# Scores of the second and third batch as row tiles, by head, with a new order of steps

## The chip, the core and the metric

The kernel runs on one core of one Trainium2 chip. The metric is the device time of one execution in microseconds (us). The engines are named as in the profile: PE (TensorE) multiplies, PEld is its loading of weights, ACT (ScalarE) and DVE (VectorE) read PE's results out of PSUM, POOL (GpSimd) and SP (SyncE) mostly issue DMAs.

## What is computed

A sliding-window causal attention (window 64) over 8 batches, 8 heads, 576 positions and a head size of 64, and after it a layer of its own kind on the 4608 tokens:

```python
scores = q @ k.T / 8, masked to 0 <= row - col < 64
x      = softmax(scores) @ v               # (8, 576, 512) -> 4608 x 512
h      = x @ w_in                          # 512 -> 2048
out    = (h - tanh(h)) @ w_out             # 2048 -> 512
```

## The kernel before

**Units.** A batch's 576 positions are 9 windows of 64. Heads go in pairs: pair `g` is batch `g // 4`, heads `g % 4` and `g % 4 + 4`; g = 0 to 3 are the first batch, 4 to 7 the second, 8 to 11 the third, and so on. The two layers work on chunks `c` of 512 tokens, 9 in all; chunk 0 needs only the first batch.

**The first three batches** are turned on PE. A pair's q or k is loaded as 96 partitions by 768 values (GpSimd's loads turn float32 into bfloat16 on the way; pair 0 comes as float32 by SP), cast or rearranged by ACT or DVE into a tile where the two heads lie side by side (`cast`), transposed on PE in six pieces (`tr`, line 253) and copied from PSUM (`put`, through `move`, line 88 on ACT and 90 on DVE). A pair that isn't cast is transposed directly, in twelve half-width pieces (line 249); pairs 2 and 3 are. k lands in `kT[g % 2]`. For the first batch q lands in `qp`, one copy with head a in partitions 0 to 63 and head b in 64 to 127, and its scores are 18 matmuls on 64 rows of the array, one for each window and head (line 286), in two groups of 4 and 5 windows; the mask is added by a product with `hide` (line 281). For the second and third batch q lands twice, in halves of `qT`, which is zero elsewhere: one matmul over 128 rows then gives a window's scores for both heads (line 292), in three groups of three windows; there the mask is a product on DVE after the exp (`masking`, line 329). Then come exp on ACT (`probs`, line 324), PV on PE (line 341 for the first batch, 354 for two pairs together later), the norm on DVE, and transposes of the result into a chunk (`x_tr`, line 403, and `x_put`).

**The other five batches** are loaded by tokens (line 159), transposed by DMAs on SP's queue (lines 164 and 172) and need no PE transposes; their scores (line 310, with 305 for the last window) are row tiles already.

**The layers.** `first_layer` is four matmuls of 512 columns for each of 16 row blocks `m` of a chunk (line 437), `tanh` on ACT (445), `subtract` on DVE (451) into `gT`; `yp_mm` is the second layer (line 480, and 473 for the last block), `y_out` copies a result from PSUM and stores it by SP (496).

**Order.** Nothing is scheduled by a program: `PLAN` is a list of steps in the order in which they are recorded, and each engine runs its own instructions in that order. A step is a letter code with numbers, looked up in `STEPS`. `lk.g`, `lq.g` load a pair's k and q; `LV`, `lv`, `lt` load v; `lr`, `qr` load k and q by tokens, `tk`, `tq` transpose them; `wi`, `wo` load the weights. `ck`, `cq` cast; `Fp.g.b` and `Ep.g.b` transpose k and q into PSUM bank `b`; `Fc` copies k, `Ec`, `Ea`, `Eb` copy q; `Rp.g.n.b` are scores of group `n`, `Rx` their exp, `M` the mask product; `Z`, `za`, `zb` copy v between halves of the partitions; `P`, `PP` are PV, `D`, `DS`, `DH`, `DR`, `DN` norms; `Xp`, `Xc` and `Y` bring x into a chunk. `H.c.m`, `A.c.m`, `G.c.m` are first layer, tanh and subtraction, `W.c.s.p` a quarter of the second layer of 128 tokens, `O.c.s` its output; `S.g` and `Sx.g` are the scores and exps of two pairs of the later batches. `U.n.b` is `n` dummy matmuls of 512 columns into bank `b`, in holes of PE's work. A last letter names the engine: p POOL, a ACT, v DVE, s SP.

The tile framework adds the waits. Three kinds matter here: a PSUM bank is written again only when its reader is done; `kT` and `qp` have two buffers, so pair g + 2 waits until pair g's scores are through; and GpSimd's DMAs take eight semaphores in turn, so one is issued only when the one eight before it has landed.

Of the kernel before, what the change touches and what calls it, by code (L numbers as in the profile page):

```python
# [15 lines left out]
def kernel(  # L16
# [200 lines left out]
    def warm_up(n, bank=5):  # L217
        w = 3 if bank == 6 else 4
        for i in range(n):
            nc.tensor.matmul(ps[:, bank, 0:128 * w], warm, warm.unsqueeze(1).to_broadcast([128, w, 128]), start=True, stop=True)  # L220
# [52 lines left out]
    def scores(g, grp, bank):  # L273
# [4 lines left out]
        if g // NP in BY_HEAD:  # L278
            if not first:
                for h in range(2):  # L280
                    nc.tensor.matmul(sp[:, :, h], ident, hide[:, h].unsqueeze(1).to_broadcast([128, n, 64]),  # L281
                                     start=True, stop=False)
            for i, j in enumerate(js):
                for h in range(2):
                    r = slice(64 * h, 64 * h + 64)
                    nc.tensor.matmul(sp[:, i, h], kt[r, 64 * j:64 * j + 128], qp[g % NKR][r, 64 * j:64 * j + 64],
                                     start=first, stop=first or i == n - 1)
            return
        if not first:
            nc.tensor.matmul(sp, ident, hide.unsqueeze(1).to_broadcast([128, n, 2, 64]), start=True, stop=False)  # L290
        for i, j in enumerate(js):
            nc.tensor.matmul(sp[:, i], kt[:, 64 * j:64 * j + 128], qT[g % NR][:, :, 64 * j:64 * j + 64],  # L292
                             start=first, stop=first or i == n - 1)
# [347 lines left out]
```

## Time and profile before

| | us |
|---|---|
| median of 3 runs | 312.18 (311.56, 312.18, 312.53) |
| the profiled execution | 311.42 |
| its span, first to last instruction | 309.7 |
| PE busy in the span | 301.3 (97%) |
| DVE, ACT, POOL busy | 183.7, 156.2, 103.0 |
| first and second layer on PE (lines 437, 480) | 140.4 and 134.3 |
| mean granted clock of PE | 0.989 of full |

Times inside the kernel are counted from the start of the span. In rows of groups the numbers after the bar are the busy time in us, the mean of one instruction in ns, and the idle time of its engine before it with what ended that. In the timeline the first two numbers are the start and the length. PE's matmuls overlap and their ends are modelled, so distances between starts tell more than lengths: a matmul of 512 columns has a length of 380 ns, but four of them take 0.86 us.

### The profile page before, as it was taken

What the parts mean: (1) busy time and instruction counts of PE and PEld (TensorE: products, weight loads), DVE (VectorE), ACT (ScalarE), POOL (GpSimd) and SP (SyncE); (2) the same over time, 40 slices, a digit from 0 to 9 for tenths busy, and PEclk for the clock granted to TensorE, in tenths of its full rate; (3) what the DMA queues carried; (4) which work ended last, traced back from release to release, by engine and by line L of the source; (5) the groups of instructions that cost most, each with busy time, mean ns of one, the idle gap of its engine ahead of it and who ended that gap; (6) DMA issues with size and microseconds to landing.
All of it is one profiled execution on the core that took longest, in us unless ns stands there. A gap on an engine that the chain in (4) does not pass through costs nothing.

```text
span 309.7 us, 6275 instructions
## 1 busy us (share of the span) xinstructions
PE 301.3 (97%) x2522; PEld 159.8 (52%) x2522; DVE 183.7 (59%) x321; ACT 156.2 (50%) x266; POOL 103.0 (33%) x139
## 2 busy tenths in 40 slices
...
GB/s 151 132 176 199 197 182 187 181 169 141 145 137 162 148 117 151 164 155 125 159 160 177 161 179 117 89 134 35 3 70 110 34 35 34 34 34 36 37 65 102
DMA packets 133436, 37.33 MB, mean 121 GB/s; under 512 B 122016, under 2 KB 127904, under 8 KB 133408
## 3 DMA queue, kind: packets, MB, share of 16 engines
...
q8 instruction: 19, 0.31, 0.4%
...
## 4 chain that ended last, share of the span: by engine, by line
PE 89%; DVE 3%; POOL 3%; DMA 2%; issue 1%; ACT 1%; POOLq 0%; ACTq 0%; DVEq 0%
PE ps L480 39%; PE ps L437 38%; PE ps L354 3%; PE ps L310 2%; DMA qall<-in_q_dram 2%; POOL vw L143 1%; PE ps L253 1%; DVE gT L451 1%; PE ps L473 1%; PE ps L292 1%; PE ps L403 1%; DVE qt L90 1%; PE ps L281 1%; POOL kall L108 1%; ACT th L445 1%
## 5 line engine op out<-in xcount | busy, mean ns | idle before, releaser
L451 DVE TENSOR_TENSOR gT<-ps,th 128x512 bf16<-128x512 f32 x144 | 97.7, 687 | 79.6 <-ACT th L445 79.0
L437 PE MATMUL ps<-xT,wi 128*128 128x512 bf16 x576 | 140.4, 380 | 0.5 <-DVE gT L451 0.2
L445 ACT ACTIVATE th<-ps 128x512 f32<-128x512 f32 x144 | 85.2, 598 | 100.0 <-PE ps L437 98.6
L480 PE MATMUL ps<-w_out_sb,gT 128*128 128x512 bf16 x560 | 134.3, 380 | 0.0
L437 PEld LDWEIGHTS <-wi 128*128 128x128 bf16 x576 | 63.0, 114 | 54.7 <-issue 0.9
L480 PEld LDWEIGHTS <-gT 128*128 128x128 bf16 x560 | 53.7, 98 | 60.9
L143 POOL DMA_DIRECT2D vw<-in_v_dram x35 | 30.5, 882 | 16.6 <-DVE q L90 9.0
L159 POOL DMA_DIRECT2D kall<-in_k_dram x25 | 21.6, 877 | 26.0 <-DMA kw<-kall 24.9
L159 POOL DMA_DIRECT2D qall<-in_q_dram x25 | 21.8, 879 | 20.9 <-DMA qw<-qall 17.5
L320 ACT ACTIVATE pt<-ps 128x1024 bf16<-128x1024 f32 (+1 forms) x30 | 23.3, 812 | 6.1 <-PE ps L310 5.9
L88 ACT ACTIVATE ysb<-ps 128x512 f32<-128x512 f32 (+1 forms) x20 | 11.6, 582 | 24.8 <-PE ps L480 19.7
L90 DVE COPY ysb<-ps 128x512 f32<-128x512 f32 (+1 forms) x17 | 11.6, 680 | 20.2 <-PE ps L480 19.5
L329 DVE TENSOR_TENSOR pt<-pt,ps 128x1152 bf16<-128x1152 bf16 x28 | 20.5, 746 | 3.2 <-ACT pt L320 2.8
L324 ACT ACTIVATE pt<-ps 128x384 bf16<-128x384 f32 (+2 forms) x32 | 16.9, 528 | 5.3 <-PE ps L292 3.4
L374 DVE TENSOR_TENSOR xs<-ps,rcp 128x384 bf16<-128x384 f32 x28 | 14.8, 550 | 0.2
L354 PEld LDWEIGHTS <-pt 128*64 128x64 bf16 x504 | 9.1, 111 | 5.1 <-issue 1.6
L354 PE MATMUL ps<-vw,pt 128*64 128x65 bf16 x504 | 10.7, 197 | 0.0
L220 PE MATMUL ps<-warm 128*128 128x512 bf16 x27 | 9.2, 498 | 1.1 <-DVE warm L197 1.1
L88 ACT ACTIVATE kt<-ps 128x576 bf16<-128x576 bf16 x10 | 6.5, 648 | 6.5 <-PE ps L253 3.5
L108 POOL DMA_DIRECT2D kall<-in_k_dram x11 | 7.3, 668 | 3.2 <-DMA wi<-in_moe_w_in_dram 1.8
...
L292 PE MATMUL ps<-qt,kt 128*128 128x128 bf16 x72 | 8.0, 219 | 0.0
...
## 6 DMA issues: line engine op xcount, KB each, us to landing
...
w_out_sb<-in_moe_w_out_dram POOLq DMA_DIRECT2D x4, 512.0 KB, 10.1
kall<-in_k_dram POOLq DMA_DIRECT2D x11, 144.0 KB, 5.2
qall<-in_q_dram POOLq DMA_DIRECT2D x11, 144.0 KB, 7.2
...
```

The source lines that it names most:

```text
L88: nc.scalar.activation(o, i, ACT.Copy)
L143: nc.gpsimd.dma_start(out=w[:, 2 * i + 1, :, 0:D] if i < NF else w[64:128, 2 * i, :, 0:D], in_=v[b, :, 128 * i:128 * i + n].rearrange("h p ...
L159: nc.gpsimd.dma_start(out=token_rows(b, n)[0:c, i], in_=(q if n == "q" else k)[b, :, 128 * i:128 * i + c].rearrange("h p d -> p h d"))
L320: nc.scalar.activation(o, sp, ACT.Exp, scale=scale)
L324: nc.scalar.activation(PT[g % NPT][:, js[0]:js[0] + len(js), :].rearrange("p i (h t) -> p i h t", h=2), sp, ACT.Exp, scale=scale)
L329: nc.vector.tensor_tensor(p, p, mask.unsqueeze(1).to_broadcast([128, 2 * NJ, 64]), ALU.mult)
L354: nc.tensor.matmul(ps[r, bank, 65 * i:65 * i + 65], PT[(g + r2) % NPT][:, j, r], vw[b % 2][:, j, p0 + r2 + NP * h, :], start=True, stop=True)
L374: nc.vector.tensor_tensor(xs[b % 2][:, 0:6, p0 + n // 2, :], ov[:, :, 0:D], sums[g][:, n].to_broadcast([128, 6, D]), ALU.mult)
L437: nc.tensor.matmul(hp, w_in_tile(ki, m), chunk_tile(c)[:, n.start // 64:n.stop // 64, ki % 2, 64 * (ki // 2):64 * (ki // 2) + 64], start=( ...
L445: nc.scalar.activation(th[:, n], hp, ACT.Tanh)
L451: nc.vector.tensor_tensor(gT[c][:, m, columns(s)], hp, th, ALU.subtract)
L480: nc.tensor.matmul(yp, gT[c][:, m, s * 128:(s + 1) * 128], w_out_sb[:, m, :], start=n == 1 and i == 0, stop=n == 4 and i == 3)
```

## The change

- The scores of the second and third batch are made as those of the first: row tiles by head, two groups of 5 and 4 windows for a pair, each head's scores in a bank of its own, from one copy of q (`qp`). `qT`, its two fills with zero (`pads_q`) and the steps `Ea` and `Eb` go. The mask stays a product after the exp.
- Pair 1 is no longer cast (`ck.1`, `cq.1`): it is transposed directly, as pairs 2 and 3 were.
- A new step `Hp` (`first_layer_part`) makes half of a first-layer block, for one half of the heads; blocks 0 to 2 of chunk 0 use it, so a block can start when two of the four pairs of x are there.
- The dummies are single steps in more places: 35 matmuls instead of 27.
- The whole list stands in a new order; which engine copies what changes too (24 of 37 y copies on ACT instead of 20).

In the new file the lines are: 215 dummies, 244 and 248 transposes, 269 `hide`, 274 row-tiled scores, 287 and 292 scores of later batches, 306 exp, 419 first layer, 491 its halves.

```diff
@@ -60,7 +60,6 @@
     WIDE = 512, 512, 1024
     w_in_sb = [const.tile([128, 4, n], BF16, name=f"wi{i}") for i, n in enumerate(WIDE)]
     w_out_sb = const.tile([128, M, d_model], BF16, name="w_out_sb")
-    BY_HEAD = (0,)
     NR, NPT, NROW = 2, 4, 3
     NKR = NR
     hidden_by_product = range(4)
@@ -72,7 +71,6 @@
     PT = [PT_all[:, i] for i in range(NPT)]
     kT = [const.tile([128, 64 + S], BF16, name=f"kt{i}") for i in range(NKR)]
     kw = [const.tile([128, NP, 64 + S], BF16, name=f"kw{i}") for i in range(2)]
-    qT = [const.tile([128, 2, S], BF16, name=f"qt{i}") for i in range(NR)]
     qp = [const.tile([128, S], BF16, name=f"qp{i}") for i in range(NKR)]
     qw = [const.tile([128, NP, S], BF16, name=f"qw{i}") for i in range(2)]
     q8 = [const.tile([128, NP, 64], BF16, name=f"q8{i}") for i in range(2)]
@@ -203,9 +201,6 @@
     def pads_k(i):
         nc.vector.memset(kT[i][:, 0:64], 0.0)
 
-    def pads_q(i):
-        nc.vector.memset(qT[i], 0.0)
-
     def pads_q8():
         for i in range(2):
             nc.vector.memset(q8[i][0:64], 0.0)
@@ -215,7 +210,7 @@
             nc.vector.memset(kw[i][:, :, 0:64], 0.0)
 
     def warm_up(n, bank=5):
-        w = 3 if bank == 6 else 4
+        w = 3 if bank == 7 else 4
         for i in range(n):
             nc.tensor.matmul(ps[:, bank, 0:128 * w], warm, warm.unsqueeze(1).to_broadcast([128, w, 128]), start=True, stop=True)
 
@@ -258,39 +253,26 @@
             move(eng, qp[g % NKR].rearrange("c (p e) -> c p e", e=E), t)
         elif which == "k":
             move(eng, kT[g % NKR][:, 64:].rearrange("c (p e) -> c p e", e=E), t)
-        else:
-            h = "ab".index(which)
-            r = slice(64 * h, 64 * h + 64)
-            move(eng, qT[g % NR].rearrange("c h (p e) -> c h p e", e=E)[r, h], t[r])
 
     def group(g, grp, bank):
-        if g // NP in BY_HEAD:
-            n = 5 - grp
-            pair = ps[:, 0:2, 0:64 * n] if bank == 0 else ps[:, 4:8:3, 0:64 * n]
-            return pair.rearrange("p h (i t) -> p i h t", t=64), range(5 * grp, 5 * grp + n)
-        return ps[:, bank, 0:384].rearrange("p (i h t) -> p i h t", i=3, h=2), range(3 * grp, 3 * grp + 3)
+        n = 5 - grp
+        pair = ps[:, 4:8:3, 0:64 * n] if bank == 4 else ps[:, bank:bank + 2, 0:64 * n]
+        return pair.rearrange("p h (i t) -> p i h t", t=64), range(5 * grp, 5 * grp + n)
 
     def scores(g, grp, bank):
         sp, js = group(g, grp, bank)
         first = g not in hidden_by_product
         kt = kT[g % NKR]
         n = len(js)
-        if g // NP in BY_HEAD:
-            if not first:
-                for h in range(2):
-                    nc.tensor.matmul(sp[:, :, h], ident, hide[:, h].unsqueeze(1).to_broadcast([128, n, 64]),
-                                     start=True, stop=False)
-            for i, j in enumerate(js):
-                for h in range(2):
-                    r = slice(64 * h, 64 * h + 64)
-                    nc.tensor.matmul(sp[:, i, h], kt[r, 64 * j:64 * j + 128], qp[g % NKR][r, 64 * j:64 * j + 64],
-                                     start=first, stop=first or i == n - 1)
-            return
         if not first:
-            nc.tensor.matmul(sp, ident, hide.unsqueeze(1).to_broadcast([128, n, 2, 64]), start=True, stop=False)
+            for h in range(2):
+                nc.tensor.matmul(sp[:, :, h], ident, hide[:, h].unsqueeze(1).to_broadcast([128, n, 64]),
+                                 start=True, stop=False)
         for i, j in enumerate(js):
-            nc.tensor.matmul(sp[:, i], kt[:, 64 * j:64 * j + 128], qT[g % NR][:, :, 64 * j:64 * j + 64],
-                             start=first, stop=first or i == n - 1)
+            for h in range(2):
+                r = slice(64 * h, 64 * h + 64)
+                nc.tensor.matmul(sp[:, i, h], kt[r, 64 * j:64 * j + 128], qp[g % NKR][r, 64 * j:64 * j + 64],
+                                 start=first, stop=first or i == n - 1)
 
     def tile_spot(r2, h, j):
         return ps[:, 3 + 2 * r2 + h, 64 * j:64 * j + 64] if j < 8 else ps[:, 7, 128 * r2 + 64 * h:128 * r2 + 64 * h + 64]
@@ -502,6 +484,14 @@
     def first_layer(c, m, s=None):
         hidden[c, m, s] = hp_mm(c, m, s)
 
+    def first_layer_part(c, m, half):
+        n = turn("h", c, m)
+        hp = ps[:, m % 2 if c > 1 else (m + c) % 3, :]
+        for i in range(2):
+            nc.tensor.matmul(hp, w_in_tile(half + 2 * i, m), chunk_tile(c)[:, :, half, 64 * i:64 * i + 64],
+                             start=n == 1 and i == 0, stop=n == 2 and i == 1)
+        hidden[c, m, None] = hp
+
     def tanh(c, m, s=None):
         hidden[c, m, s] = squash(s, hidden[c, m, s])
 
@@ -509,7 +499,7 @@
         g_sub(c, m, s, *hidden.pop((c, m, s)))
 
     STEPS = dict(
-        i=make_ident, u=make_warm, mv=pads_v, mt=pads_k, mq=pads_q, mk=pads_kw, mz=pads_q8, tz=tail_q, U=warm_up, h=make_hide, n=make_mask, N=put_mask,
+        i=make_ident, u=make_warm, mv=pads_v, mt=pads_k, mk=pads_kw, mz=pads_q8, tz=tail_q, U=warm_up, h=make_hide, n=make_mask, N=put_mask,
         lk=lambda g, e: load(g, "k", e), lq=lambda g, e: load(g, "q", e),
         LK=lambda b: load_all(b, "k"), LQ=lambda b: load_all(b, "q"),
         lt=load_v_tail, lv=load_v, LV=load_rows,
@@ -517,10 +507,10 @@
         ck=lambda g, e: cast(g, "k", e), cq=lambda g, e: cast(g, "q", e),
         qr=load_q, tq=tr_q, S=tile_scores, Sx=tile_probs,
         Fp=lambda g, k: tr(g, "k", k), Ep=lambda g, k: tr(g, "q", k),
-        Fc=lambda g, k, e: put(g, "k", k, e), Ea=lambda g, k, e: put(g, "a", k, e), Ec=lambda g, k, e: put(g, "c", k, e), Eb=lambda g, k, e: put(g, "b", k, e),
+        Fc=lambda g, k, e: put(g, "k", k, e), Ec=lambda g, k, e: put(g, "c", k, e),
         Rp=scores, Rx=probs, M=masking, za=cross_low, zb=cross_high, Z=cross_rows,
         P=pv, D=norm, DS=norm_sums, DH=norm_half, PP=pv_pairs, DR=recip_pairs, DN=norm_pairs, Xp=x_tr, Xc=x_put, Y=x_dma,
-        H=first_layer, A=tanh, G=subtract, W=yp_mm, O=y_out)
+        H=first_layer, Hp=first_layer_part, A=tanh, G=subtract, W=yp_mm, O=y_out)
 
     def play(script):
         for word in script.split():
@@ -528,86 +518,85 @@
             STEPS[what](*[ENG[a] if a in ENG else int(a) for a in args])
 
     PLAN = """
-        mt.1 mt.0 lk.1.p lq.1.p i u mv.0 LV.0.0 lk.5.p U.1 lk.0.s U.1 lq.0.s lq.3.p U.4 LV.0.3 LV.0.4 h LV.0.1
-        cq.0.a U.13 mq.0 mv.1 U.1.3 ck.1.a cq.1.v mq.1 Fp.1.2 Ep.1.3 LV.0.2 Fc.1.2.a U.2 ck.0.v Fp.0.2 lk.3.p
-        Ec.1.3.v Fc.0.2.v Rp.1.1.4 Ep.0.3 Ec.0.3.v Rx.1.1.4 lq.2.p Rp.1.0.0 lv.1.1.1 lk.2.p lq.5.p Rx.1.0.0 U.4
-        Rp.0.1.4 Rp.0.0.0 ck.5.a lk.4.p Z.0 Rx.0.1.4 Ep.3.3 Rx.0.0.0 Fp.3.2 lv.1.0.0 lk.6.p lq.4.p P.0 Fc.3.2.a
-        Ec.3.3.v lk.7.p D.0 Ep.2.3 Rp.3.1.4 Ec.2.3.a Rp.3.0.0 U.1.2 Rx.3.1.4 Fp.5.3 wi.0 Fp.2.2 cq.5.a Fc.5.3.v
-        P.1 lv.1.1.0 ck.4.v D.1 Rx.3.0.0 Fc.2.2.a Ep.5.3 Rp.2.1.4 Eb.5.3.a lq.7.p lv.1.0.1 wi.1 Rp.2.0.0
-        Rx.2.1.4 P.3 Rx.2.0.0 Ea.5.3.v wi.2 Fp.4.3 lq.6.p P.2 Xp.0.0.1.2 cq.4.v Fc.4.3.a Rp.5.0.4 D.3 DS.2
-        Xp.0.0.0.3 Rx.5.0.4 DH.2.0 Xc.0.0.1.2.a Xc.0.0.0.3.v DH.2.1 Xp.0.1.0.3 Xc.0.1.0.3.a Xp.0.1.1.2 Rp.5.1.4
-        Ep.4.3 Xc.0.1.1.2.v ck.6.v Ea.4.3.v Eb.4.3.v H.0.0 H.0.1 lv.1.2.0 A.0.0 Rx.5.1.4 lk.8.p cq.7.v lv.1.2.1
-        lq.8.p H.0.2 A.0.1 G.0.0 n lv.1.3.1 Rp.4.2.4 ck.7.v G.0.1 H.0.3 Rx.4.2.4 Rp.5.2.4 wo.0 A.0.3 Rx.5.2.4
-        G.0.3 Fp.7.3 H.0.4 Rp.4.0.4 A.0.2 N G.0.2 H.0.6 Rx.4.0.4 Fc.7.3.a M.5 A.0.4 za.1.0.v G.0.4 H.0.5 A.0.6
-        lv.1.3.0 Fp.6.3 Rp.4.1.4 A.0.5 Fc.6.3.a G.0.5 H.0.7 zb.1.0.p Ep.7.3 A.0.7 G.0.6 H.0.8 Ea.7.3.a G.0.7
-        cq.6.v A.0.8 H.0.9 Eb.7.3.v G.0.8 za.1.1.p Rx.4.1.4 H.0.10 A.0.9 zb.1.1.p lt.1 M.4 Rp.7.0.4 Ep.6.3
-        A.0.10 H.0.11 Eb.6.3.a Rx.7.0.4 G.0.9 wo.2 G.0.10 H.0.12 A.0.11 lq.9.p wo.1 Rp.7.2.4 Rx.7.2.4 H.0.13
-        wo.3 Ea.6.3.v G.0.11 A.0.12 cq.8.v lk.9.p Rp.6.1.4 H.0.14 G.0.12 Rx.6.1.4 Ep.8.3 ck.8.v H.0.15 A.0.14
-        Rp.6.2.4 lq.11.p LV.2.0 G.0.14 mz za.1.2.v lk.10.p Rx.6.2.4 PP.4 A.0.15 zb.1.3.p DR.4 Rp.6.0.4 DN.4.2
-        W.0.0.0 Ea.8.3.a LV.2.2 Eb.8.3.a za.1.3.v G.0.15 W.0.0.2 Rx.6.0.4 Fp.8.3 lq.10.p DN.4.1 cq.9.v Rp.7.1.4
-        W.0.1.2 W.0.1.0 Fc.8.3.a DN.4.0 zb.1.2.a M.6 Rx.7.1.4 M.7 Rp.8.0.4 Ep.9.3 Rx.8.0.4 A.0.13 PP.6 LV.2.1
-        Ea.9.3.a Eb.9.3.a W.0.0.1 Rp.8.2.4 W.0.1.1 Xp.1.0.0.3 Rx.8.2.4 DR.6 LV.2.3 G.0.13 W.0.1.3 Xc.1.0.0.3.a
-        Rp.8.1.4 W.0.0.3 O.0.1.v Xp.1.0.1.3 Xc.1.0.1.3.v DN.6.1 O.0.0.v ck.10.v ck.9.a W.0.3.3 Fp.9.3 lk.11.p
-        Fc.9.3.a W.0.3.0 Rx.8.1.4 DN.6.0 DN.6.2 W.0.2.0 W.0.2.3 cq.10.a Rp.9.2.4 lr.3.2 Rx.9.2.4 LV.2.4 lr.4.0
-        qr.3.3 W.0.3.1 Xp.1.1.0.3 qr.4.1 qr.3.1 Xc.1.1.0.3.a Rp.9.1.4 W.0.3.2 O.0.3.a W.0.2.2 M.8 Z.2 lr.3.4
-        Xp.1.1.1.3 W.0.2.1 Xc.1.1.1.3.a LV.3.3 H.1.0 O.0.2.v Ep.10.3 A.1.0 Rx.9.1.4 tq.3.3 Eb.10.3.v H.1.1 H.1.2
...
+        mz u U.1.3 U.1.1 lq.3.p U.1.7 U.1.7 U.1.3 U.4.5 mv.0 lq.1.p lk.3.p lk.1.p lk.0.s lk.2.p U.4.6 mv.1 mt.0
+        LV.0.3 ck.0.v LV.0.1 mk U.4.6 U.1.2 lq.0.s i cq.0.v U.1.6 U.1.4 U.1.3 Ep.0.6 U.1.5 U.1.7 Fp.0.2 U.1.5
+        Ep.1.4 LV.0.0 LV.0.2 Ec.1.4.a lq.2.p lq.7.p Fp.3.4 Fp.1.3 U.1.0 lq.4.p h lq.5.p Ec.0.6.a U.1.6 Fc.1.3.a
+        U.1.7 Fc.0.2.v U.1.7 mt.1 Rp.0.1.1 Rx.0.1.1 Rp.1.0.6 Rp.1.1.1 U.1.3 Rx.1.0.6 Fp.2.5 Fc.3.4.v Ep.2.6
+        Rx.1.1.1 Ep.3.0 Ec.3.0.v Rp.0.0.4 Z.0 U.1.1 U.1.2 Rp.3.1.2 LV.0.4 Fc.2.5.a Ec.2.6.a U.1.0 lk.4.p
+        Rp.2.0.0 lk.5.p lq.9.p cq.5.v Rx.0.0.4 Rx.3.1.2 P.1 Rp.2.1.2 D.1 cq.4.v wi.0 Rx.2.0.0 ck.4.a Rx.2.1.2
+        Rp.3.0.0 Rx.3.0.0 P.0 Ep.4.2 U.1.7 P.2 ck.5.a D.0 Ec.4.2.a Fp.4.4 lv.1.1.0 lk.6.p Fc.4.4.a U.1.5
+        lv.1.0.0 P.3 DS.2 DH.2.0 Xp.0.0.0.0 D.3 Rp.4.1.2 Ep.5.7 lv.1.1.1 Xp.0.0.1.4 DH.2.1 Xp.0.1.0.6
+        Xc.0.0.0.0.a n lv.1.3.0 Rx.4.1.2 Xp.0.1.1.1 Rp.4.0.2 Xc.0.1.0.6.a Xc.0.0.1.4.v ck.6.v Hp.0.0.0 N U.1.6
+        Fp.6.5 Rx.4.0.2 Fp.5.2 Fc.5.2.a Xc.0.1.1.1.v cq.7.v Ec.5.7.v Hp.0.0.1 Hp.0.1.1 Fc.6.5.v Hp.0.1.0
+        Rp.5.1.4 lq.6.p Rp.5.0.5 wi.1 lk.7.p lv.1.0.1 A.0.0 A.0.1 zb.1.1.p wi.2 Rx.5.1.4 Rx.5.0.5 cq.6.v
+        Hp.0.2.0 Hp.0.2.1 A.0.2 G.0.0 G.0.1 lk.8.p M.4 lv.1.3.1 H.0.3 H.0.4 G.0.2 lq.8.p Ep.6.5 ck.7.v H.0.5
+        cq.9.v A.0.3 A.0.4 wo.0 Fp.7.7 Ec.6.5.a A.0.5 G.0.3 lt.1 Rp.6.0.5 G.0.4 Ep.7.4 Ec.7.4.a lv.1.2.1
+        Rx.6.0.5 H.0.6 Fc.7.7.v Rp.7.0.3 Rx.7.0.3 M.5 A.0.6 H.0.7 A.0.7 G.0.5 za.1.0.a Rp.7.1.3 Rp.6.1.6 wo.2
+        Ep.9.5 G.0.6 lv.1.2.0 wo.3 za.1.1.p H.0.8 G.0.7 A.0.8 H.0.9 Rx.7.1.3 zb.1.0.p wo.1 ck.8.v G.0.8 lq.11.p
+        H.0.10 zb.1.3.p A.0.9 Rx.6.1.6 G.0.9 H.0.11 lk.9.p A.0.10 G.0.10 H.0.12 A.0.11 A.0.12 G.0.11 lr.3.0
+        lk.10.p lq.10.p LV.2.2 G.0.12 Ec.9.5.a Fp.8.3 H.0.13 H.0.14 cq.8.a M.7 Fc.8.3.a lr.3.1 H.0.15 Ep.8.3 M.6
+        A.0.14 A.0.15 PP.4 G.0.14 W.0.0.0 Ec.8.3.a G.0.15 A.0.13 DR.4 W.0.1.0 DN.4.1 DN.4.0 zb.1.2.v G.0.13
+        lr.3.3 W.0.0.2 Rp.8.0.3 Rp.8.1.5 za.1.3.a lk.11.p W.0.1.2 DN.4.2 Rx.8.1.5 qr.3.3 za.1.2.v LV.2.0 LV.2.4
+        PP.6 DR.6 DN.6.2 DN.6.0 DN.6.1 LV.2.1 LV.2.3 Xp.1.0.1.1 Rx.8.0.3 W.0.0.3 Xp.1.0.0.4 W.0.1.3 Xp.1.1.0.7
+        Xp.1.1.1.6 W.0.0.1 qr.3.4 Xc.1.1.0.7.v O.0.0.a qr.3.2 Xc.1.0.0.4.v W.0.1.1 tq.3.4 Xc.1.0.1.1.v ck.9.v
+        M.8 Xc.1.1.1.6.a W.0.2.3 Fp.9.3 W.0.2.1 W.0.2.2 Fc.9.3.v O.0.1.v Rp.9.1.5 Rp.9.0.3 W.0.2.0 W.0.3.3
+        cq.10.a Rx.9.0.3 Rx.9.1.5 ck.10.a W.0.3.0 H.1.0 W.0.3.2 W.0.3.1 O.0.2.v A.1.0 G.1.0 M.9 O.0.3.v Fp.10.5
...
```

113 lines of the change are left out of this document (56 added, 57 removed).

## The prediction

> **What bounds the kernel now.** I read the page first (PE 97% busy), then the busy time by stage, the chain of waits in order of time, and the timeline of the first 50 us. The stages below are cut where PE's timeline shows the first matmul of the first layer, the first of the second layer, and the first scores of batch 3.
>
> ```profile
> 27.93 2.75 PE L437 MATMUL ps<-xT,wi 128*128 128x512 bf16 x12
> 46.62 1.89 PE L480 MATMUL ps<-w_out_sb,gT 128*128 128x512 bf16 x8
> 94.12 0.22 PE L305 MATMUL ps<-q,kw 128*128 128x64 bf16 x2
> ...
> 0.00:27.93 27.93, 23.19 (x315) 13.45 (x316) 14.54 (x33) 15.13 (x23) 24.02 (x40) 0.88 1.29 159
> 27.93:46.62 18.69, 18.23 (x163) 10.85 (x161) 16.49 (x33) 14.19 (x28) 11.72 (x20) 1.00 1.26 194
> 46.62:94.10 47.48, 47.48 (x408) 26.63 (x406) 33.88 (x66) 30.96 (x58) 30.94 (x38) 1.00 1.96 159
> 94.10:306.30 212.20, 212.20 (x1644) 108.83 (x1643) 118.79 (x193) 95.63 (x157) 36.33 (x44) 1.00 0.84 100
> 306.30:309.70 3.40, 0.22 (x4) 0.05 (x1) 0.00 (x0) 0.28 (x1) 0.00 (x0) 1.00 0.34 119
> ```
>
> The columns are length, then busy time of PE, PEld, DVE, ACT, POOL, then PE's clock. From 46.62 PE has no hole. So the time is: when the first second-layer matmul starts (46.62), plus the PE work left then (259.7), plus holes that a new order makes, plus the tail (3.4). Before 46.62 PE is full of dummies and waits, and the chain tells what it waits for:
>
> ```profile
> 3.37 0.87 POOL vw L143
> 5.48 1.63 POOL vw L143 x2
> 7.76 0.94 POOL hide L226
> 9.55 0.90 POOL vw L143
> 11.05 5.96 DMA qall<-in_q_dram
> 17.06 0.69 PE ps L249 x12
> ```
>
> That is GpSimd issuing v loads, making `hide`, issuing more, and at 11.05 the load of pair 2's q, which lands at 17.0 (the twelve half-width transposes at 17.06 are Ep.2). The start hangs on GpSimd's order of issue.
>
> **Part 1: the start, up to the first first-layer matmul.**
>
> ```profile
> L108 POOL DMA_DIRECT2D qall<-in_q_dram x11 | 7.2, 658 | 0.9 <-DVE gT L451 0.9
> L143 POOL DMA_DIRECT2D vw<-in_v_dram x35 | 30.5, 882 | 16.6 <-DVE q L90 9.0 <-DMA vw<-in_v_dram 1.9 <-PE ps L253 1.8
> qall<-in_q_dram POOLq DMA_DIRECT2D x11, 144.0 KB, 7.2
> L88 ACT ACTIVATE kt<-ps 128x576 bf16<-128x576 bf16 x10 | 6.5, 648 | 6.5 <-PE ps L253 3.5 <-PE ps L249 2.9
> L88 ACT ACTIVATE kb<-kall 96x768 bf16<-96x768 bf16 x3 | 2.5, 835 | 0.5 <-DMA kall<-in_k_dram 0.5
> L324 ACT ACTIVATE pt<-ps 128x640 bf16<-128x640 f32 x4 | 2.8, 699 | 0.4 <-PE ps L286 0.3
> L324 ACT ACTIVATE pt<-ps 128x512 bf16<-128x512 f32 x4 | 2.4, 597 | 1.3 <-PE ps L286 1.2
> L445 ACT ACTIVATE th<-ps 128x512 f32<-128x512 f32 x144 | 85.2, 598 | 100.0 <-PE ps L437 98.6 <-DVE gT L451 0.6 <-DVE pt L329 0.5
> L451 DVE TENSOR_TENSOR gT<-ps,th 128x512 bf16<-128x512 f32 x144 | 97.7, 687 | 79.6 <-ACT th L445 79.0
> ...
> 25.66 0.64 POOL L108 DMA_DIRECT2D kall<-in_k_dram  x1 [1.84 <-DMA wi<-in_moe_w_in_dram]
> ```
>
> In the new order lq.2 stands behind five q/k loads, four v loads and `ident`, ahead of `hide`. At 0.66 and 0.88 us each and about 0.5 for `ident`, from the same first issue (about 1.4), it is issued at 1.4 + 3.3 + 3.5 + 0.5 = 8.7 to 8.9, some 2.2 us earlier than at 11.05. With the 5.96 us of the old one's landing it is there at 14.8; with the median of its kind (7.2) at 16.1. I take 14.8: as many q/k loads and one v load less are ahead of it on the same DMA engines.
>
> Until then nothing is later than it: the dummies run to about 8.2, Ep.0 follows, and Rp.0.1 waits for `hide`, now made behind lq.7 and lq.4 (ready at 12.2 instead of 8.7). That is 2.9 us after the first scores of the old order (9.4), but Rp.0.1, Rp.1.0, Rp.1.1 and Fp.2 then take PE to 14.7, just q2's arrival. Ep.2, Ep.3 and Rp.0.0 take 0.3 + 0.3 + 0.6, and a hop to ACT 0.25: at 16.2 ACT may overwrite kT[0]. From there ACT works without a gap: four copies (Fc.2, Ec.2, Ec.4, Fc.4) at 0.65, five exps (three of 640 columns at 0.70, two of 512 at 0.60) and two casts (ck.4, ck.5) at 0.84 make 7.6 us, to 23.8. Then Rp.4.1, Ep.5 and one Xp on PE (0.8 with hops), Xc on DVE (0.65): the first half-layer Hp.0.0.0 starts at about 25.8 instead of 27.93. PV and norms run inside those 7.6 us; w_in's first piece has as many q/k and v loads ahead of it as before and two small v loads fewer; its landing then ended the wait of a later load at 25.66, so about 24.5 now.
>
> **Part 2: from there to the second layer.** Up to A.0.14 ACT has 14 tanhs (8.4; A.0.13 and A.0.15 come later), four wide and three narrow exps (4.6), five copies (3.2), one cast and one v copy (1.5): 17.7 us from 26.0, with 1.3 of waits (0.8 of them Fc.5's for its transposes) 45.0; G.0.14 on DVE (0.69) frees bank 2, and W.0.0.0 starts at 45.75. Old: 46.62. **Term: -0.9 us.** So 2.1 us gained at the start shrink, because ACT, 14.19 busy of 18.69 in this stretch before, becomes its bound.
>
> **Part 3: PE work left at the first W.** First and second layer, PV and chunk transposes are equal in number. The order of the new program has 30 cast transposes left instead of 42 (-0.5 us at 0.042, a count of six lasting 0.25 below), 72 row-tiled score matmuls instead of 39 full ones, and 55 changes of the array's shape instead of 46.
>
> ```profile
> 9.39 0.38 PE L281 MATMUL ps<-hide,ident 128*128 128x256 bf16 x2
> 9.70 0.29 PE L286 MATMUL ps<-qp,kt 64*128 64x64 bf16 x8
> 9.93 0.43 PE L253 MATMUL ps<-ident,qb 96*128 96x96 bf16 x6
> 10.19 0.44 PE L281 MATMUL ps<-hide,ident 128*128 128x320 bf16 x2
> 10.56 0.32 PE L286 MATMUL ps<-qp,kt 64*128 64x64 bf16 x10
> 10.81 0.39 PE L220 MATMUL ps<-warm 128*128 128x512 bf16 x1
> ...
> 70.37 0.33 PE L292 MATMUL ps<-qt,kt 128*128 128x128 bf16 x3
> 70.54 1.89 PE L437 MATMUL ps<-xT,wi 128*128 128x512 bf16 x8
> 72.36 0.76 PE L354 MATMUL ps<-vw,pt 128*64 128x65 bf16 x36
> ...
> 42.63 0.86 PE ps L437 x4
> ```
>
> Starts to starts: three full score matmuls 0.17 (70.37 to 70.54). Eight row-tiled 0.23 and ten 0.25, the way out included: 0.0145 each and 0.1 for the way out. Eight first-layer matmuls before PV's column tiles 1.82 instead of 8 x 0.216 = 1.73: 0.1 for the way in. So a pair's scores cost 18 x 0.0145 + 0.2 a burst = 0.66 in two bursts and 0.46 where both stand together (pairs 8 and 9), against 9 x 0.056 = 0.51. From the first W on: 72 x 0.0145 - 39 x 0.056 = -1.1, nine changes +0.9, transposes -0.5: **-0.7 us**.
>
> The Trainium skill (TensorEngine Tiling (Array Packing), Tiling Modes) says that changing the tiling mode drains TensorE; the rows agree with 0.1 us a change, and without that charge this term would be -1.6. The same page's table gives a speedup of up to 2x for a dimension of at most 64, a gain of about 1.1 in this term where the rows, changes included, leave -0.2.
>
> **What costs nothing.** The two fills of qT (DVE, idle then) go; sixteen half copies of q become eight whole ones and 24 exps of 384 columns sixteen wider ones. After 46.62 ACT and DVE are busy 30.96 and 33.88 of 47.48 us, so this saves no time there; if they had been the bound it would be some 5 us (eight copies of 0.65). Four y copies go from DVE to ACT, under the same cover. Eight dummies more fill holes. Single dummies wait for their bank's reader, so each delays what follows on PE at most 0.22 us.
>
> **Holes later.** Before there are none, so the new order can only be worse: between 0 and 1.5 us (a late bank or two in each of the next chunks, 0.1 to 0.3 at a time). I take 0.4: my walk from W.0.0.0 to batch 3 finds 0.1 at Xp.1.1, 0.1 at Rp.10.0, 0.2 elsewhere.
>
> **Sum:** -0.9 - 0.7 + 0.4 = -1.2 us. The profiled execution took 311.42 (309.7 span and 1.7 around it), the median is 312.18; on it the forecast is 311.0.
>
> **Rivals.**
>
> *q2 no earlier where it matters.* It lands at 16.1 and everything on ACT shifts by 1.2: 0.0 in sum, 312.2, with more holes 312.9. Against: the DMA engines are less loaded ahead of it. For: early landings are uneven.
>
> *The clock falls (slower).*
>
> ```profile
> 15.35 0.45 PE L249 MATMUL ps<-ident,kall 96*64 96x96 bf16 x12 [2.05 <-DMA kall<-in_k_dram]
> ...
> 13.07:16.46 3.39, 1.06 (x44) 0.82 (x38) 1.89 (x3) 1.22 (x2) 3.39 (x6) 1.00 1.41 172
> 16.46:19.88 3.42, 2.94 (x42) 1.43 (x37) 1.30 (x3) 1.89 (x4) 2.91 (x5) 0.50 1.43 180
> 19.88:23.29 3.41, 3.41 (x56) 2.55 (x55) 2.21 (x5) 2.05 (x5) 3.41 (x6) 0.50 1.18 173
> ```
>
> After a stretch with PE busy 1.06 of 3.39 us the clock was halved for two such stretches. The new order keeps PE busy, by my walk, 2.0 us or more in each such stretch from 9.7 to 26 (least between 16.5 and 19.9, with Rp.3.1, Rp.2.0, P.1, Rp.2.1 and one dummy). Where the limit lies between 1.06 and that, nothing shows. If it falls, 4.7 us of PE work in two stretches becomes 9.4 in 6.8: +2.6, so 313.6. The Trainium skill (TensorE: Matmul & The Clock Gate, Why this matters for your kernels) asks only for no idle gap over about 3 us between bursts; by that this rival is out. Here it fell after an idle gap of 2.05 us, the longest before it (the row at 15.35), so the row decides and I keep the rival.
>
> *Batch 3 is not ready (slower).* Its first scores move from 94.1 to about 88.2 (20 N=512 matmuls fewer stand ahead of S.12).
>
> ```profile
> 83.53 2.50 SPq L164 DMA_TRANSPOSE kw<-kall  x2
> ...
> kw<-kall SPq DMA_TRANSPOSE x25, 4.9
> ```
>
> The last of k's transposes was issued at 84.8 and with the median landing came at 89.7. In the new order ten transposes stand behind the fourth y store (about 64) at 1.25 us each, with waits for loads to 76 and landed by 82. If SP's queue comes no earlier than before, S.12 waits 1.5, and with loads behind them up to 4: 311.0 + 1.5 to 4, middle 313.5.
>
> *The holes before the first W go too.* ACT loses half of its 1.3 and no later hole comes: 312.18 - 0.9 - 0.7 - 0.6 = 310.0.
>
> **How the numbers follow.** Forecast 0.50 (310.5 to 312.1), q2 late 0.14, clock 0.13, batch 3 late 0.10, better 0.09, other holes 0.04 (313). No change is within 0.3%, 0.94 us. Of the forecast's 0.50, 0.31 lies below 311.2, so 0.31 + 0.09 = 0.40 faster; its other 0.19 and 0.10 of q2's case make 0.29 same; the rest, 0.31, is slower. The range takes in the better case and the clock: 310.0 to 313.8.
>
> **What would show it.** Right: q2's Ep.2 at 14.8, first L491 matmul at 25.8, first second-layer matmul at 45.7, clock 1.00 from 7 us on, S.12 at 88 with no wait, PE full from 46. Wrong: a 0.5 in the clock's digits between 9 and 27 us; W.0.0.0 later than 46.6; PE idle time in front of line 287 or 419 after 50 us.

## The result: 10.7 us slower, and the profile after

The changed kernel took 322.8 us (median of 4 runs, 319.67 to 324.69); the kernel before, timed beside it, 312.1 (311.56 to 312.53): 1.031 times as long, 95% interval 1.024 to 1.039. The slowest of the four, 324.69, lies over 1.5% above the fastest and is left out of this ratio. The forecast was 311.0 and its range ended at 313.8. The profiled execution has a span of 320.8 us.

The digits of the page, PE and its clock in 40 slices of 8.02 us:

```profile
PE   8899999999999969999999269999999999999996
PEclk9999999999999999999999759999999999999999
```

Two dents, counted from 0 at slice 14 (a little after 112 us) and slices 22 and 23 (from 176), the second with a lower clock. Both lie where the prediction expected a full PE. The list of waits names them (engine and line, then what it waited for: total, times, longest; line 292 is the scores of later batches, 419 the first layer, 336 PV):

```profile
PE ps L292 <- DMA qw<-qall: 6.8, 1, 6.8
PE ps L419 <- DMA xT<-xs: 4.6, 2, 2.8
...
PE ps L336 <- DVE vw L148: 0.5, 1, 0.5
PE ps L292 <- DMA kw<-kall: 0.3, 1, 0.3
```

`qw` and `xT` are written by SyncE's transposes: batch 6's q ahead of the scores S.24, chunk 3's and chunk 5's x ahead of the first layer. Cut at the first half of the first layer, the first second-layer matmul and the two dents, by stage (columns as in the prediction):

```profile
0.00:24.70 24.70, 22.31 (x340) 12.89 (x341) 12.65 (x33) 13.17 (x21) 21.71 (x39) 1.00 1.40 168
24.70:43.62 18.92, 18.88 (x210) 10.90 (x205) 16.28 (x30) 16.82 (x31) 13.06 (x20) 1.00 1.28 199
43.62:115.29 71.67, 70.91 (x698) 38.02 (x698) 50.43 (x89) 38.85 (x67) 32.72 (x40) 1.00 1.59 146
115.29:118.13 2.84, 0.00 (x0) 0.00 (x0) 1.71 (x3) 0.00 (x0) 2.84 (x5) 1.00 1.70 100
118.13:178.35 60.22, 60.22 (x506) 31.16 (x506) 36.44 (x60) 28.38 (x48) 31.22 (x37) 1.00 2.05 149
178.35:191.50 13.15, 4.59 (x43) 2.24 (x44) 1.38 (x2) 2.19 (x3) 0.88 (x1) 0.61 2.01 151
191.50:320.80 129.30, 126.00 (x825) 63.45 (x823) 60.67 (x96) 54.15 (x91) 0.00 (x0) 1.00 0.24 60
```

The start is better than forecast: the second layer begins at 43.62 (46.62 before, 45.75 forecast). Everything is lost behind it. From there to the end 277.2 us pass instead of 263.1. The ledger of the span, 320.8 - 309.7 = +11.1: start -3.0; PE waits 0.5 + 0.3 + 2.8 + 6.8 + 1.8 = +12.2 (1.8 is the second of the two waits for `xT`, 4.6 - 2.8); PE's own work -0.4 (the same stretch takes 262.68 us in o_m11y below, where PE never waits in it; 263.08 before); the remaining 2.3 is the clock, at 0.50 from 181.2 to 191.4 (nearly all of PE's 4.59 busy us in the stretch from 178.35 fall into it, and half of them is 2.3).

Why the transposes were late shows when PE's and SyncE's timelines are laid side by side. The kernel before, SyncE's queue (start, length, what):

```profile
165.62 1.22 SPq L172 DMA_TRANSPOSE qw<-qall  x1
169.79 5.19 SPq L422 DMA_TRANSPOSE xT<-xs  x2
```

and PE, at S.24 and at the first layer of chunk 5:

```profile
174.62 0.22 PE L305 MATMUL ps<-q,kw 128*128 128x64 bf16 x2
178.89 1.03 PE L437 MATMUL ps<-xT,wi 128*128 128x512 bf16 x4
```

The changed kernel, SyncE's queue:

```profile
111.54 3.15 SPq L404 DMA_TRANSPOSE xT<-xs  x2
...
176.38 1.28 SPq L170 DMA_TRANSPOSE qw<-qall  x1
178.38 8.04 SPq L404 DMA_TRANSPOSE xT<-xs  x2
```

and PE:

```profile
118.13 1.89 PE L419 MATMUL ps<-xT,wi 128*128 128x512 bf16 x8 [2.84 <-DMA xT<-xs]
...
178.12 0.22 PE L287 MATMUL ps<-q,kw 128*128 128x64 bf16 x2
188.03 3.56 PE L419 MATMUL ps<-xT,wi 128*128 128x512 bf16 x8 [1.78 <-DMA xT<-xs]
```

Before, batch 6's last transpose is issued 9.0 us ahead of S.24, and chunk 5's x 9.1 us ahead of its first layer. After, the first comes 1.7 us ahead. The second is issued at 178.38; without the wait for q PE would have been ready for it at about 178.9 (an estimate: S.24 started at 178.12, and in the kernel before the first layer follows it 0.8 us later), 0.5 us behind the issue. Chunk 3's x had 5.8 us and now has 3.75 (issued at 111.54, PE ready for it at 115.29). How long such a transpose takes differs with what else is under way. Issues by line with the median time to landing, changed kernel, between 99 and 111 us, where GpSimd issues no load:

```profile
kw<-kall SPq DMA_TRANSPOSE x5, 2.4
qw<-qall SPq DMA_TRANSPOSE x3, 2.4
```

and between 171 and 181, where it issues eight:

```profile
kw<-kall SPq DMA_TRANSPOSE x2, 8.8
qw<-qall SPq DMA_TRANSPOSE x2, 9.5
xT<-xs SPq DMA_TRANSPOSE x2, 10.9
```

Two things on GpSimd's queue feed that crowd (its timeline, changed kernel):

```profile
139.23 0.88 POOL L157 DMA_DIRECT2D qall<-in_q_dram  x1 [14.15 <-DMA qw<-qall]
172.20 1.75 POOL L141 DMA_DIRECT2D vw<-in_v_dram  x2 [6.70 <-PE ps L336]
```

At 139.23 a load of batch 7's q (qr.7.1) has waited 14.15 us for a transpose of batch 5, with batch 5's v and batch 6's rows behind it. At 172.20 batch 7's v starts, released by PV of batch 5, the same PV that Y.5 (the transposes of batch 5's x) waits for: the loads, and the transposes that PE needs next, are set off by the same event.

### The profile page after: what moved, and what is told of

It reads as the page before. It is cut to its first block, busy times and chain, and to the rows that moved or that the text cites. A ratio compares the mean times of both kernels' runs of the same rounds, so it can differ in the third digit from the quotient of the medians.

```text
span 320.8 us, 6454 instructions
## 1 busy us (share of the span) xinstructions
PE 302.9 (94%) x2614; PEld 158.7 (49%) x2614; DVE 179.6 (56%) x309; ACT 153.6 (48%) x258; POOL 102.4 (32%) x139
## 3 DMA queue, kind: packets, MB, share of 16 engines
q1 hardware_dynamic: 42224, 18.88, 31.6%
## 4 chain that ended last, share of the span: by engine, by line
PE 78%; DMA 12%; ACT 3%; SPq 2%; DVE 2%; issue 1%; POOL 1%; ACTq 0%
PE ps L462 34%; PE ps L419 31%; DMA xT<-xs 5%; PE ps L215 3%; DMA vw<-in_v_dram 3%; PE ps L336 2%; DMA qall<-in_q_dram 2%; DMA kw<-kall 2%; PE ps L292 2%; SPq L170 1%; PE ps L248 1%; PE ps L455 1%; ACT pt L306 1%; DVE gT L433 1%; ACT th L427 1%
## 5 line engine op out<-in xcount | busy, mean ns | idle before, releaser
L141 POOL DMA_DIRECT2D vw<-in_v_dram x35 | 30.2, 874 | 20.3 <-PE ps L336 17.4
L157 POOL DMA_DIRECT2D kall<-in_k_dram x25 | 21.6, 867 | 33.3 <-DMA kw<-kall 22.8
L86 ACT ACTIVATE ysb<-ps 128x512 f32<-128x512 f32 (+2 forms) x24 | 13.9, 579 | 29.0 <-PE ps L462 28.0
L157 POOL DMA_DIRECT2D qall<-in_q_dram x25 | 21.8, 881 | 16.2 <-DMA qw<-qall 14.1
L306 ACT ACTIVATE pt<-ps 128x512 bf16<-128x512 f32 (+1 forms) x24 | 14.8, 651 | 5.0 <-PE ps L274 4.9
L88 DVE COPY ysb<-ps 128x512 f32<-128x512 f32 x13 | 8.9, 685 | 11.0 <-PE ps L462 11.0
L292 PE MATMUL ps<-qw,kw 64*128 64x64 bf16 x340 | 7.5, 195 | 7.1 <-DMA qw<-qall 6.8
L215 PE MATMUL ps<-warm 128*128 128x512 bf16 (+1 forms) x35 | 11.8, 470 | 1.3 <-DVE warm L195 1.3
L336 PE MATMUL ps<-vw,pt 128*64 128x65 bf16 x504 | 10.7, 197 | 0.5 <-DVE vw L148 0.5
L292 PEld LDWEIGHTS <-kw 64*128 64x128 bf16 x340 | 6.3, 98 | 7.7 <-issue 6.8
L86 ACT ACTIVATE qp<-ps 128x576 bf16<-128x576 bf16 x9 | 5.7, 645 | 8.5 <-PE ps L244 8.2
L88 DVE COPY kt<-ps 128x576 bf16<-128x576 bf16 x6 | 4.5, 750 | 8.6 <-PE ps L248 4.7
```

The lines of the kernel that those rows point to most:

```text
L86: nc.scalar.activation(o, i, ACT.Copy)
L141: nc.gpsimd.dma_start(out=w[:, 2 * i + 1, :, 0:D] if i < NF else w[64:128, 2 * i, :, 0:D], in_=v[b, :, 128 * i:128 * i + n].rearrange("h p ...
L157: nc.gpsimd.dma_start(out=token_rows(b, n)[0:c, i], in_=(q if n == "q" else k)[b, :, 128 * i:128 * i + c].rearrange("h p d -> p h d"))
L292: nc.tensor.matmul(tile_spot(r2, h, j), kw[b % 2][r, n + 2 * h, 64 * j:64 * j + 128], qw[b % 2][r, n + 2 * h, 64 * j:64 * j + 64], start=T ...
L336: nc.tensor.matmul(ps[r, bank, 65 * i:65 * i + 65], PT[(g + r2) % NPT][:, j, r], vw[b % 2][:, j, p0 + r2 + NP * h, :], start=True, stop=True)
```

## The experiments

Each is built on the kernel its diff names; words are those of the plan.

**1. Moving the load that blocks GpSimd (a_qr71).**

```diff
- qr.6.1 qr.7.1 LV.5.0 lr.6.0 ... qr.6.3 qr.6.2 lr.7.1
+ qr.6.1 LV.5.0 lr.6.0 ... qr.6.3 qr.6.2 qr.7.1 lr.7.1
```

> The changed kernel with one word moved: the load of batch 7's second row block of q (qr.7.1) stands on GpSimd's queue behind batch 5's v and batch 6's first k and q loads instead of ahead of them. Theory 1 (order of issue): GpSimd stood idle for 14.1 us up to 139.2 at qr.7.1, which waits for a transpose of batch 5, and nine loads that could have gone waited behind it; with the word moved they are issued from about 125, batch 6's transposes start at about 147 instead of 159, the scores of pair 24 find their q, the wait of 6.79 us at 178 and the one of 1.78 behind it go, and the clock, halved from 181 to 191, stays at 1.00: 322.7 - 8.6 - 2.2 = 312. Rival (the DMA engines or SyncE's queue of transposes are simply too slow for a PE that is 3 us ahead): the same bytes come no sooner, the hole shrinks by 2 us at most: 320 to 322.5.

Measured 322.89 us, ratio to before 1.033 (1.029 to 1.036): no gain. PE's waits:

```profile
PE ps L419 <- DMA xT<-xs: 8.9, 2, 6.0
PE ps L292 <- DMA qw<-qall: 1.2, 1, 1.2
```

The wait for q fell from 6.8 to 1.2 (and that is at another place, S.20), as theory 1 said. But Y.5, issued at 178.94, landed only at 188.13, and the first layer waited 6.0 us for it instead. Theory 1 was right in the block and wrong in its 312; the time lies just above the rival's 320 to 322.5. That Y.5 took 9.2 us is not SyncE's own queue, which had stood empty from 176.5 to 178.94. The block on GpSimd was real; behind it stood the next wait, at the same place in time.

**2. A later release at Y.3 (a_lr63).**

```diff
- tk.4.3 lr.6.3 LV.4.4 tk.4.0 ... LV.5.0 lr.6.0
+ tk.4.3 lr.6.0 LV.4.4 tk.4.0 ... LV.5.0 lr.6.3
```

> The changed kernel with two loads exchanged on GpSimd's queue: lr.6.0, which waits for the transpose that lands last (112.65), comes where lr.6.3 stood, which was released at 111.37. The row of loads behind it then starts about 1.2 us later against the transpose Y.3 that the first layer of chunk 3 waits for (issued at 111.54, landed 118.09). Theory (Y.3 lands late because the loads start 0.4 us behind its issue): it lands within 4 us of its issue and PE's wait of 2.84 us at 115.3 falls below 1; about 320.5. Rival (Y.3 is simply issued too late behind nine other transposes): wait still 2 to 3 us, 322 to 323.

Measured 325.34 us (ratio 1.037 to 1.045), and the experiment fails as a test: the exchange put lr.6.0 ahead of tk.4.0, which reads the rows that it overwrites, so in this kernel one block of batch 4's k is batch 6's. The load then waited for nothing of the kind and went at 95, the loads behind it at 109, and they met the last transposes of batch 4 as well (PE waited 2.6 us for `kw`, and later 6.6 for chunk 5's x). Nothing follows for Y.3.

**3. The loads from batch 4 on in another order (a_loads).**

```diff
- LV.4.3 lr.6.3 LV.4.4 lr.5.4 qr.5.3 lr.5.0 qr.5.0 qr.7.4 lr.5.3 ... qr.7.1 LV.5.0 ...
+ LV.4.3 LV.4.4 lr.5.4 qr.5.3 lr.5.0 qr.5.0 lr.5.3 lr.5.2 qr.5.2 qr.5.1 lr.5.1
+ (behind tk.4.0) lr.6.0 lr.6.3 LV.5.0 LV.5.3 LV.5.1 qr.6.4 qr.6.1 LV.5.2 LV.5.4 ... qr.7.4 qr.7.1 lr.7.1
```

> The changed kernel with GpSimd's loads from batch 4 on in another order and all else kept: ten loads of batch 4 and 5 that wait for nothing go at 89 to 98 instead of behind a waiting load of batch 6; batch 6's first loads and batch 5's v come after the last transpose of batch 4; the loads of batch 7 that wait for batch 5's transposes (qr.7.4, qr.7.1) come last. Theory 1: no wait of PE on a DMA above 0.5 us after 90, clock 1.00 throughout, so the holes (2.84, 6.79, 1.78) and the 2.2 of the halved clock go: 322.7 - 13.6 = 309, 3 under the kernel before. Rival (row-tiled scores leave less PE work to hide the transfers, so DMA is the bound): at least 5 us of the holes stay, 314 or more.

Measured 318.88 us (ratio 1.017 to 1.028): 4 us better, where theory 1 had 13.6 (309) and its rival 314 or more. What is left is in the main chunk 5's x (4.9), with 2.1 for batch 3's k at S.12 and 1.3 for chunk 3's x:

```profile
PE ps L419 <- DMA xT<-xs: 6.2, 2, 4.9
```

**4. The reverse on the kernel before (b_qr73).**

```diff
- LV.5.1 (behind lr.6.0) ... LV.5.3 ... LV.5.2 LV.5.0 LV.5.4 ... lr.6.4 ... qr.6.3 ... qr.7.3
+ qr.7.3 LV.5.1 LV.5.3 lr.6.4 LV.5.2 LV.5.0 LV.5.4 qr.6.3
```

> The reverse, on the kernel before: seven loads (batch 5's v and the first k and q loads of batch 6) are put behind qr.7.3, which waits for a transpose of batch 5 until 144. Nothing else is changed: scores, casts, order of PE are the old ones. Theory 1: those loads come some 20 us later, batch 6's transposes slip, and PE waits in front of pair 24's scores (174.6) or at batch 5's v: 314 to 320. Rival (the holes need the new scores or the earlier PE): still 312.1 within 0.6.

Measured 325.57 us (ratio 1.040 to 1.045): +13.5, more than theory 1 had. VectorE waits for batch 5's v and holds up everything queued behind it. Its list of waits, and PE's timeline:

```profile
DVE vw L149 <- DMA vw<-in_v_dram: 16.3, 2, 12.7
```

```profile
158.09 2.29 PE L437 MATMUL ps<-xT,wi 128*128 128x512 bf16 x5 [11.33 <-DVE gT L451]
```

So with the old scores and the old order of PE's work as much is lost when one waiting load is put ahead of seven others, though by another wait: for v, not for transposes. A loss of this size doesn't need the new scores.

**5. Batch 7's loads held until Y.5 has landed (h_y5).**

```diff
+    def hold(c):
+        nc.gpsimd.tensor_copy(held, chunk_tile(c)[:, 7, 0, 0:64])
- lr.7.2 LV.7.0
+ lr.7.2 K.5 LV.7.0
```

> The changed kernel with one small instruction added on GpSimd ahead of batch 7's v loads (it copies 64 columns of chunk 5's x, so it waits until the transpose Y.5 has landed); the eight loads behind it come after Y.5 instead of just ahead of it. Theory 2 (a row of loads that is issued right ahead of a transpose makes it land in 8 to 15 us instead of 2.4): Y.5 lands within 5 us of its issue (9.5 before) and batch 6's last transpose of q within 6 (8.7), PE's two waits from 178 on fall from 8.57 to 2 to 4 in sum and the clock stays at 1.00: 314 to 317 instead of 322.7. Rival (the transposes are slow by the bytes already under way or by SyncE's own queue): waits of 7 or more remain, 320 to 323.

Measured 315.0 us (ratio 1.006 to 1.018), inside theory 2's range; 7.8 us back by eight loads that come 11.5 us later. Y.5 landed in 4.7 us and batch 6's last transpose in 4.1 (issues between 176 and 183, then PE's timeline; lines are one higher here):

```profile
xT<-xs SPq DMA_TRANSPOSE x2, 4.7
...
qw<-qall SPq DMA_TRANSPOSE x1, 4.1
```

```profile
183.19 3.48 PE L420 MATMUL ps<-xT,wi 128*128 128x512 bf16 x8 [2.08 <-DMA xT<-xs]
```

Y.5's issue on SyncE's queue:

```profile
178.34 4.03 SPq L405 DMA_TRANSPOSE xT<-xs  x2
```

Waits of 0.4 and 2.1 us are left: PE was ready for x at 181.11, 2.8 us behind the issue, and the first of the two transposes needed 4.8. The clock still fell, against theory 2: those eight matmuls take 3.48 us. This profiled execution is the slowest of the four (317.87); in it the clock fell behind the wait at chunk 3's x too, 2.59 us long here.

**6. Both (h_loads): a_loads, with K.3 ahead of lr.6.0 (behind Y.3) and K.5 ahead of LV.7.0.**

> The loads in the order of a_loads (318.9 us), with two such holds: behind Y.3 ahead of the loads of batch 6, and behind Y.5 ahead of those of batch 7's v. Theory 2: PE's waits of 1.28 and 0.27 at Y.3 and 4.92 at Y.5 go and the clock stays at 1.00: 318.9 - 1.5 - 4.9 - 1.7 = 310.8, between 308.5 and 313 by how late the first batch-3 transposes and w_in are in the run. Rival (another wait takes their place, as Y.5's took that of the scores of pair 24): 315 or more.

Measured 310.96 us, ratio to before 0.996 (0.993 to 0.999), where 310.8 was expected. PE's waits for DMAs behind 60 us:

```profile
PE ps L420 <- DMA xT<-xs: 1.5, 1, 1.5
...
PE ps L293 <- DMA kw<-kall: 1.2, 2, 0.8
```

The new order of PE's work, with nothing but GpSimd's queue rearranged and two small copies put into it, is 11.8 us faster than the changed kernel. Y.5 has 3.7 us here (issued at 174.44, used at 178.11), and PE doesn't wait for it. The 1.5 is Y.3's: it took 5.2 us to land although no load was issued or under way beside it.

**7. Old order behind the third batch's scores (o_m11), and from pair 18 (o_s20).**

```diff
- (changed plan, all words)
+ (changed plan up to M.11 or up to S.18, then the words that are left in the order of the plan before)
```

> The changed kernel up to the masking of the last pair of the third batch (word M.11 of the plan), so with the new start, the scores by head in both batches, pair 1 uncast, halves and dummies; every later step in the old kernel's order. Theory 3 (the time was lost by the new order of the steps behind that point and nothing else of the change): no wait of PE on a DMA above 1 us after 60, the 3.0 us of the earlier first second-layer matmul are kept: 312.1 - 3.0 - 0.2 = 309, 308.5 to 310.5. Rival (a PE that is 3 us ahead, with fewer cycles of scores, must wait for the DMAs in any order): 312 or more.

> The changed kernel up to the scores of pair 18 (127.6; 126.6 in the old kernel), and every later step in the old order. Theory 3: the waits at 87 (0.3) and 115 (2.8) stay as they are, those of 6.79 and 1.78 at 178 to 188 and the halved clock are gone; from pair 18 on the time of the old kernel: 312.1 + 1.0 = 313, 312 to 314.5. Rival (the waits at 178 come from what lies before pair 18, the lateness of batch 5's loads): 317 or more.

o_m11: 311.96 us (ratio 0.998 to 1.004), 309 expected. No wait for a DMA above 0.5 us after 60, as theory 3 had it. The second layer started at 44.12, 2.5 us earlier than before, but this gain was lost behind it, and by its time alone the run would fit the rival (312 or more). The list of waits shows the largest part:

```profile
PE ps L462 <- ACT ysb L86: 1.7, 3, 1.0
```

Second-layer matmuls wait for copies of y on ScalarE: the mixture kept the new plan's choice of engine for each copy with the old plan's order. o_s20: 316.19 us (1.008 to 1.019; its profiled execution 314.79), 313 expected, 314.5 at most, and 317 or more by the rival: between the two. It has the same mixture and the same 1.7. Its waits at 178 to 188 and the low clock behind them are gone, the 2.9 at Y.3 is there.

**8. The mixture mended (o_m11y):** as o_m11, with the old engines and banks from M.11 on.

> As o_m11 (311.96 us), but from M.11 on also the old kernel's engines for the copies of y and its banks for chunk 2's transposes. Theory 3: what ate the 2.5 us in o_m11 were the waits of second-layer matmuls for y copies on ScalarE (1.7 in the list of waits) that only the mixture of old order and new engines made; they go: 312.1 - 2.5 - 0.2 = 309.4, 308.6 to 310.4, with no wait of PE above 0.6 us after 46. Rival (the earlier PE meets another limit in the old order): 311 or more.

Measured 308.96 us, ratio 0.993 (0.990 to 0.996): 3.0 us under the kernel before and 13.8 under the changed one, with all of the changed scores, casts, halves and dummies. Its stages from the first half-layer on, and then all that PE waits for in the whole execution:

```profile
24.70:43.62 18.92, 18.88 (x210) 10.89 (x205) 16.17 (x30) 16.82 (x31) 11.87 (x19) 1.00 1.28 193
43.62:306.30 262.68, 259.31 (x2070) 133.91 (x2069) 152.34 (x257) 119.68 (x200) 69.49 (x83) 1.00 1.04 112
```

```profile
PE ps L215 <- DVE warm L195: 1.3, 1, 1.3
PE ps L244 <- ACT qp L86: 0.7, 1, 0.7
PE ps L248 <- ACT pt L306: 0.2, 1, 0.2
```

All three waits lie ahead of 27 us. The DMAs are as crowded as ever, Y.5 takes 6.7 us to land, but the order allows it 9.1. This is the fastest version measured. Engines and banks went back together, so which of them gave back how much isn't separated.

**9. What of the start matters (s_q2, s_half, s_dum), on o_m11y.**

```diff
- lq.2.p lq.7.p Fp.3.4 Fp.1.3 U.1.0 lq.4.p h lq.5.p        (s_q2)
+ lq.7.p Fp.3.4 Fp.1.3 U.1.0 lq.4.p h lq.5.p lq.2.p
- Hp.0.0.0 ... Hp.0.0.1 Hp.0.1.1 ... Hp.0.1.0 ... Hp.0.2.0 Hp.0.2.1   (s_half)
+ H.0.0 H.0.1 ... H.0.2
- the ten words U.1.x behind h                             (s_dum)
```

> As o_m11y, but pair 2's q load (lq.2) is issued behind the making of hide and three more loads, at about 12 us instead of 8.8. If the start hangs on this load, as the prediction had it: its transposes start at about 17 instead of 14.8, the first half of the first layer at 26.5 instead of 24.6 and the first second-layer matmul 1.5 to 2 later: 311. Rival (ScalarE bounds the stretch behind it, so the lateness is made up): 309.4 to 310.

> As o_m11y, but the first three first-layer tiles whole, where their second halves stood. If the halves bring the start forward: first first-layer matmul at 26.2 instead of 24.6, first second-layer matmul 0.5 to 1.3 later, 310 to 310.7. Rival (the halves only fill PE's spare time ahead of work that ScalarE paces): within 0.4 of o_m11y.

> As o_m11y, but without the eleven single dummy matmuls behind the making of hide (2.4 us of PE between 11 and 26). If the clock goes by the share of busy time in 3.4 us, as the prediction's rival had it, it falls to 0.50 for some 7 us between 14 and 27: 312. Rival (only a gap of some 3 us without a matmul lowers it, and none is that long): clock 1.00, within 0.5 of o_m11y.

s_q2: 311.57 us (ratio to before 0.997 to 1.002), 2.6 over o_m11y. s_half: 309.31 (0.989 to 0.995). s_dum: 309.20 (0.988 to 0.994). Nine of o_m11y's twelve runs lie between 308.17 and 309.98, so halves and single dummies (s_dum leaves out ten of the 35 matmuls, not the eleven that its expectation names) can't be told from nothing, although in s_half's profile the second layer starts at 44.51 instead of 43.62. The early q load can be told. In s_q2's profile its transposes start at 16.95, as expected, but the first half of the first layer at 28.71 (26.5 expected) and the second layer at 47.63. The clock was halved meanwhile (PE's timeline, then the row of windows over the halved stretch):

```profile
16.95 1.17 PE L244 MATMUL ps<-ident,qall 96*64 96x96 bf16 x24 [2.75 <-DMA qall<-in_q_dram]
```

```profile
15.40:22.20 6.80, 5.25 (x61) 2.65 (x61) 2.65 (x4) 2.32 (x4) 6.65 (x11) 0.50 1.30 167
```

Nine of s_q2's ten runs have a mean clock of 0.989 to 0.994 and take 310.9 to 313.3; the tenth, at 1.00, takes 309.51. So, as far as one run tells, the lateness of q2 alone costs half a microsecond (the rival's 309.4 to 310), and the clock that falls in the gap costs the other two. In o_m11y it is the same: the nine runs above are at 0.998 or more, the three others, at 0.994 to 0.995, take 312.0 to 312.4.

In s_dum, the stretch of the profiled execution with the least PE work, of the kind that the prediction's clock rival feared:

```profile
15.80:19.20 3.40, 2.56 (x56) 1.59 (x56) 2.51 (x6) 3.38 (x7) 3.16 (x6) 1.00 1.18 166
```

The clock stays at 1.00. With 2.56 of 3.40 us busy, this stretch is fuller than the 2.0 that the prediction counted even with dummies, so a limit between 1.06 and 2.56 isn't excluded. Two of its other three runs have a mean of 0.993 and 0.989 and take 308.87 and 309.59, so wherever it fell in those, it cost nothing that shows.

## Why the prediction was wrong

**The step that failed is "Holes later: between 0 and 1.5, I take 0.4".** It measured 12.2, and the clock that fell with it 2.3. The prediction took those holes to be late banks, because it walked the new order from W.0.0.0 only to batch 3. SyncE's and GpSimd's queues were counted through batch 3 and no further, though the diff moves loads and transposes of batches 4 to 7 as well. The trace of before held what was needed: transposes land there after 2.4 to 12 us, and at the three places above PE left them 5.8 to 9.1 us. The new plan has tq.6.0 on SyncE's queue shortly ahead of S.24 on PE's (1.7 us as measured); a walk to the end would have met it, though what it would have made of the distance is not shown. That it is the order of steps behind M.11, and not the scores, o_m11y shows; that within it the distance of transposes from their use and the loads set off beside them count, h_y5 and h_loads show.

**The rival "Batch 3 is not ready" named the right mechanism at the wrong place.** Its own point, S.12, came at 86.49 (88.2 forecast) and waited 0.29 us for its last transpose, not 1.5 to 4. The same thing three batches later, at S.24, cost 6.8, and the clock fell in that wait.

**Part 1 was right in its events and 1.1 us too slow in its sum.** q2's load was issued at 8.78 (8.7 to 8.9 forecast), its transposes began at 14.83 (14.8), ScalarE began its stretch at 16.18 (16.2). But the first half of the first layer started at 24.70, not 25.8:

```profile
16.18 0.65 ACT L86 ACTIVATE kt<-ps 128x576 bf16<-128x576 bf16 x1 [1.24 <-PE ps L274]
16.73 0.65 ACT L86 ACTIVATE qp<-ps 128x576 bf16<-128x576 bf16 x1
17.26 1.80 ACT L306 ACTIVATE pt<-ps 128x640 bf16<-128x640 f32 x3
19.08 0.84 ACT L86 ACTIVATE kb<-kall 96x768 bf16<-96x768 bf16 x1
```

The second copy starts 0.55 us after the first, which lasts 0.65, and three exps of 0.70 take 1.80 together. The eleven instructions took 6.6 us to the end of the last one (22.80), where the sum of durations gave 7.6: 0.09 each. The Trainium skill (ScalarE: Activation LUTs, What ACT_TABLE_LOAD costs) states just this, an overlap of about 93 ns between ACTIVATEs back to back; the trace agrees, and the prediction added durations all the same.

**Part 2 failed by the same mis-sizing.** By that 0.09, its 28 instructions are some 2.5 us too many in the 17.7 (an estimate); ScalarE was busy 16.82 of 18.92, PE 18.88, so ScalarE was not the bound that turned 2.1 into 0.9. The stretch took 18.92 instead of 19.95. The term was -3.0, not -0.9. s_q2 shows that most of it hangs on the early q load (2.6 by medians), and there mostly by the clock, as far as s_q2's one run at 1.00 tells: it was at 0.50 from 16.46 to 23.29 before (the windows in the prediction), and the new start, with no gap of PE above 0.2 us from 11.0 to there, avoids it. No run of the kernel before has a mean clock above 0.994; nine of o_m11y's twelve have 0.998 or more. The prediction showed that row, used it for a rival, and left out that its end was a gain.

**Part 3 was near:** -0.4 measured (262.68 against 263.08), -0.7 forecast.

**The clock rival was wrong at its place and right in kind:** 1.00 from 9 to 181 us, then halved by the DMA wait. At the start nothing was lost even without the dummies (s_dum, 309.2 where 312 stood against it), but the thinnest stretch there has 2.56 us of work, not the 2.0 that it feared.
